# Linear attention and a routed expert per sequence: output tiles split by feature parity, expert weights kept in fixed slots with a conditional load, first expert product in halves, and another order list

## The chip, the cores and the metric

The kernel runs on one core of one Trainium2 chip. The metric is the device time of one execution in microseconds (us); lower is better. A core has a matmul engine (TensorE, PE in the profile, with weight loads as PEld), a vector engine (VectorE, DVE), a scalar engine (ScalarE, ACT), GpSimd (POOL), which issues all the loads here, and SyncE (SP), which issues the stores. Each engine takes its instructions in the order in which the program gives them to it.

## The reference, cut to what matters

For each of 8 sequences: 8 heads of linear attention (k^T v, then q times that), a root-mean-square norm over each head's 64 features, then a mean over the 576 positions that chooses one of 8 experts, and that expert's two products.

```python
batch, n_heads, seq, head_dim = (8, 8, 576, 64)
kv = np.einsum('bhsd,bhse->bhde', k, v)
out = np.einsum('bhsd,bhde->bhse', q, kv)
rms = np.sqrt(np.mean(out * out, axis=-1, keepdims=True) + 1e-06)
x = out / rms * g_norm                          # to (8, 576, 512)
logits = x.mean(axis=1) @ w_gate                # (8, 8 experts)
e_idx = np.argmax(logits, axis=1)
h = np.maximum(x[mask] @ w1[e], 0.0)            # 512 -> 1024
out[mask] = gate_w[mask, None, None] * (h @ w2[e])   # 1024 -> 512
```

With the inputs as they are drawn, the eight sequences choose experts 4, 4, 7, 6, 5, 1, 3, 1. Sequence 1 so repeats the expert of the one before it, and sequence 7 that of sequence 5.

## The kernel before, in words

All inputs are float32 in memory and are turned into float16 on the way in by the loads (GpSimd's queue); sums stay in float32. The program is a list of small steps, ORDER (lines 18 to 47), run in that order at build time; a step's name is two letters, then the sequence and an index. Every engine gets its instructions in the order of the list, so the list is the schedule; nothing is reordered later.

Loads: `lq` (line 93), `lk` (97), `lv` (103). The values v go into one of three block-diagonal buffers `vbd`, two heads to a block, with zeros that `zero_v` (129) writes once. `wl` (247) reads the chosen expert's index into a GpSimd register and loads both weight matrices, 1 MB each as float16, into a pool with three buffers.

Attention of one sequence: `tr` (134) transposes q, 18 matmuls; `te` (146) copies the result out of PSUM as qT (VectorE). `kv` (157) forms k^T v with 36 matmuls of 128 rows, 64 columns and 128 streamed columns, half of which are the zeros of `vbd`; `kc` (167) copies it to float16 (three VectorE casts). `ou` (176), for each of four pairs of heads `c`, multiplies with q on four 64x64 quarters of the array; its streamed operand steps through qT by 128 elements (256 bytes) from one column to the next:

```python
s["qT"][rs].rearrange("p j (h n) -> p h n j", h=H)[:, 2 * c + h]
```

`sq` (188, ScalarE) squares the result, `oc` (194, VectorE) copies it, `me` (199) takes the mean over the features with a matmul, `ln` (206, ScalarE) does a logarithm and an exponential, `xt` (213, VectorE) scales into xT. There are four of each per sequence. `ga`, `gb`, `gc` (223 to 245) form the logits and the index; `gb` is a small float32 matmul that needs all four `xt`. `ge` (258) forms the gate.

Expert of one sequence: `m1` (268) has eight steps of eight matmuls of 288 columns into a two-bank PSUM tile, `re` (279, ScalarE) takes 576 columns out of it; `m2` (286) has four steps of eight matmuls of 512 columns and one of 32 small ones (128 rows by 32 columns, line 301); `ev` (306, VectorE) scales two of the four at a time and SyncE stores them.

PSUM is one pool with two tags, "a" (attention) and "m" (expert), each of two tiles of two banks.

The list does the attention of sequences 0 and 1 first, then in each stage the expert of sequence b with the attention of sequence b + 2 woven between its steps, and at the end the experts of 6 and 7 alone. Loads of sequence b + 2 stand behind the weights of sequence b on GpSimd's queue, and those wait for the index of sequence b. At a stage's end `gb` of sequence b + 2 stands on TensorE's queue behind all of `m2` but its last step.

Of the kernel before, what the change touches and what calls it, by code (L numbers as in the profile page):

```python
# [24 lines left out]
sq21 oc21 re04 me20 m105 ln20 xt20 re05 me21 m106 ln21 xt21 re06 ou22 sq22 m107 oc22 re07 ou23
sq23 m200 oc23 m201 me22 ln22 ev00 xt22 me23 m202 ln23 m203 xt23 ga2 ev01 gb2 m204 gc2 wl2 ev02
ge2 lk4 lv40 lv41 lq4 m110 tr30 te30 re10 tr31 te31 m111 tr32 re11 te32 kv30 m112 kv31 re12 kc3
ou30 m113 sq30 oc30 re13 ou31 m114 sq31 oc31 re14 me30 m115 ln30 xt30 re15 me31 m116 ln31 xt31
re16 ou32 sq32 m117 oc32 re17 ou33 sq33 m210 oc33 m211 me32 ln32 ev10 xt32 me33 m212 ln33 m213
xt33 ga3 ev11 gb3 m214 gc3 wl3 ev12 ge3 lk5 lv50 lv51 lq5 m120 tr40 te40 re20 tr41 te41 m121  # L30
# [12 lines left out]
m251 me72 ln72 ev50 xt72 me73 m252 ln73 m253 xt73 ga7 ev51 gb7 m254 gc7 wl7 ev52 ge7 m160 re60
m161 re61 m162 re62 m163 re63 m164 re64 m165 re65 m166 re66 m167 re67 m260 m261 ev60 m262 m263
ev61 m264 ev62 m170 re70 m171 re71 m172 re72 m173 re73 m174 re74 m175 re75 m176 re76 m177 re77
m270 m271 ev70 m272 m273 ev71 m274 ev72
"""


@with_exitstack  # L50
def kernel(
    ctx: ExitStack,
    tc: tile.TileContext,
    q: bass.AP,
    k: bass.AP,
    v: bass.AP,
    g_norm: bass.AP,
# [10 lines left out]
    P = 128  # L68
# [290 lines left out]
```

## Time and profile before

| what | value |
|---|---|
| median of 3 runs | 249.75 us (249.34 to 250.88) |
| the profiled execution, its own time | 249.76 us |
| its span, first to last instruction | 248.0 us |
| time around the span | 1.76 us |
| TensorE busy | 196.9 us, 79% |
| VectorE / ScalarE busy | 111.6 us, 45% / 105.1 us, 42% |
| read from memory / written | 61.88 MB / 9.44 MB |

The profile shows one execution. Busy time of TensorE counts a matmul to its modelled end, so runs of matmuls overlap. In a windows view, the DMA columns give the mean busy share of the 16 DMA engines and what they moved (loads count as float16 there). The chain of waits is followed back from the last instruction, at each step to what released it.

### The profile page before, as it was taken

Reading aid. Unit: us, or ns where it says so; the run is one execution under the profiler, and the core shown is the slowest. Engines: PE = TensorE matmul, PEld = TensorE weight load, DVE = VectorE, ACT = ScalarE, POOL = GpSimd, SP = SyncE. Lnnn points to the kernel's source line nnn. Section 1 sums busy time; section 2 is a strip of 40 time slices with the busy share of each in tenths; the row PEclk is TensorE's granted clock in tenths of the full one; section 3 lists DMA queues with packets and bytes.
Section 4 is the critical chain, followed back from the end, with each engine's and each line's share of the span. In section 5 each row is a group of like instructions: output and inputs, shape, how many; then the busy total and the mean of one; then the engine's idle time right before and its main releaser. Section 6 shows DMA issues by size and latency. Waiting matters only on the chain.

```text
span 248.0 us, 4062 instructions
## 1 busy us (share of the span) xinstructions
PE 196.9 (79%) x1664; PEld 123.0 (50%) x1664; DVE 111.6 (45%) x235; ACT 105.1 (42%) x177; POOL 32.8 (13%) x54
## 2 busy tenths in 40 slices
PE   0355366358899889978998899889997999999990
PEld 0231151036554656464646564557455645957840
DVE  6625535532446535573357236733574358022031
ACT  2007405711484249413951385328542654622600
POOL 7100060041000500032002300140002000200000
PEclk9999999999999999999999999999999999999998
DMA  4996049999992699949995999599969902995023
GB/s 37 201 207 128 0 74 215 204 161 211 207 183 85 145 215 207 245 121 209 208 220 176 183 208 214 204 168 210 213 204 170 202 1 104 202 215 201 2 87 107
DMA packets 20644, 40.65 MB, mean 164 GB/s; under 512 B 2194, under 2 KB 11410, under 8 KB 20626
## 3 DMA queue, kind: packets, MB, share of 16 engines
q0 software_dynamic: 16128, 30.94, 69.1%
q1 hardware_dynamic: 4498, 9.46, 10.6%
q8 instruction: 13, 0.21, 0.3%
q14 instruction: 5, 0.04, 0.0%
HBM read 61.88 MB, written 9.44 MB: 288 GB/s over the span
## 4 chain that ended last, share of the span: by engine, by line
PE 61%; DMA 12%; DVE 11%; ACT 9%; issue 3%; POOL 2%; DVEq 0%; POOLq 0%
PE ps_m L275 27%; PE ps_m L294 14%; DMA qt<-in_q_dram 7%; PE ps_a L183 6%; DMA kt<-in_k_dram 5%; ACT ln L209 4%; ACT ln L211 4%; PE ps_a L162 4%; PE ps_a L144 3%; DVE xT L218 2%; PE ps_m L301 2%; PE ps_a L203 2%; DVE qT L149 2%; DVE kv L173 1%; DVE kv L172 1%
## 5 line engine op out<-in xcount | busy, mean ns | idle before, releaser
L275 PE MATMUL ps_m<-xT,w 128*128 128x288 f16 x512 | 74.0, 293 | 0.4 <-DVE ot L312 0.4
L275 PEld LDWEIGHTS <-w 128*128 128x128 f16 x512 | 56.0, 116 | 16.4 <-issue 10.5
L281 ACT ACTIVATE hT<-ps_m 128x576 f16<-128x576 f32 x64 | 41.5, 648 | 46.4 <-PE ps_m L275 46.3
L294 PE MATMUL ps_m<-w,hT 128*128 128x512 f16 x256 | 57.6, 379 | 0.0
L218 DVE SCALAR_TENSOR_TENSOR xT<-o,gcol,ln 128x576 f16<-128x576 f32 x32 | 26.2, 818 | 30.6 <-ACT ln L211 30.6
L294 PEld LDWEIGHTS <-hT 128*128 128x128 f16 x256 | 24.5, 98 | 30.2 <-issue 2.8
L312 DVE TENSOR_SCALAR ot<-ps_m,gates 128x1024 f32<-128x1024 f32 x16 | 20.5, 1281 | 34.3 <-PE ps_m L294 34.3
L191 ACT ACTIVATE sq<-ps_a 128x576 f16<-128x576 f32 x32 | 20.4, 650 | 36.0 <-PE ps_a L183 36.0
L197 DVE COPY o<-ps_a 128x576 f32<-128x576 f32 x32 | 23.9, 756 | 20.6 <-ACT sq L191 20.6
L183 PE MATMUL ps_a<-qT,kv 64*64 64x288 f16 x128 | 26.0, 651 | 7.7 <-DVE kv L171 4.2
L209 ACT ACTIVATE ln<-ps_a,eps 128x576 f32<-128x576 f32 x32 | 23.5, 734 | 19.2 <-PE ps_a L203 19.2
L252 POOL DMA_DIRECT2D w<-in_moe_w_dram x8 | 6.0, 754 | 178.9 <-PE ps_a L144 86.6
L144 PE MATMUL ps_a<-ident,qt 128*128 128x128 f16 x144 | 14.4, 253 | 17.1 <-DMA qt<-in_q_dram 10.3
L211 ACT ACTIVATE ln<-ln 128x576 f32<-128x576 f32 x32 | 21.9, 685 | 1.0
L144 PEld LDWEIGHTS <-qt 128*128 128x128 f16 x144 | 11.9, 116 | 19.2 <-DMA qt<-in_q_dram 10.8
L203 PE MATMUL ps_a<-sq,ones 128*128 128x288 f16 x64 | 13.9, 320 | 5.3 <-DVE o L197 5.2
L162 PE MATMUL ps_a<-vbd,kt 128*64 128x128 f16 x288 | 13.1, 250 | 5.7 <-DVE qT L152 3.1
L149 DVE COPY qT<-ps_a 128x1024 f16<-128x1024 f16 x16 | 11.0, 690 | 11.6 <-PE ps_a L144 11.6
L162 PEld LDWEIGHTS <-kt 128*64 128x64 f16 x288 | 11.3, 129 | 8.0 <-issue 4.5
L183 PEld LDWEIGHTS <-kv 64*64 64x64 f16 x128 | 4.7, 109 | 19.4 <-issue 7.3
L171 DVE CAST kv<-ps_a 128x256 f16<-128x256 f32 x8 | 3.4, 424 | 22.2 <-PE ps_a L162 22.2
L264 ACT ACTIVATE lg<-lg 128x8 f32<-128x8 f32 x8 | 1.7, 208 | 26.3 <-DVE lg L261 26.3
(36 smaller groups left out, 89.5 us busy)
## 6 DMA issues: line engine op xcount, KB each, us to landing
w<-in_moe_w_dram POOLq DMA_DIRECT2D x16, 1024.0 KB, 10.7
out_dram<-ot SPq DMA_DIRECT2D x16, 512.0 KB, 2.8
qt<-in_q_dram POOLq DMA_DIRECT2D x8, 576.0 KB, 18.6
vbd<-in_v_dram POOLq DMA_DIRECT2D x16, 288.0 KB, 15.9
kt<-in_k_dram POOLq DMA_DIRECT2D x8, 576.0 KB, 15.0
out_dram<-ol SPq DMA_DIRECT2D x32, 32.0 KB, 2.1
gcol<-in_g_norm_dram SPq DMA_DIRECT2D x1, 0.5 KB
wg<-in_moe_w_gate_dram SPq DMA_DIRECT2D x1, 16.0 KB, 8.0
```

The costliest lines, as they stand in the source:

```text
L144: nc.tensor.transpose(dst, s["q"][:, j, :], cs["ident"])
L162: nc.tensor.matmul(s["pk"][64 * g:64 * g + 64, 0, n * P:(n + 1) * P], s["k"][:, c, j, :], vbd[b % 3][:, c, :, j * Dh:(j + 1) * Dh], start= ...
L183: nc.tensor.matmul(po[64 * h:64 * h + 64, r, 0:HS], s["kv"][rs, col + 64 * h:col + 64 * h + 64], s["qT"][rs].rearrange("p j (h n) -> p h n ...
L191: nc.scalar.activation(t.rearrange("p (i n) -> p i n", i=2), s["po", c][:, :, 0:HS], AF.Square)
L197: nc.vector.tensor_copy(t.rearrange("p (i n) -> p i n", i=2), s["po", c][:, :, 0:HS])
L209: nc.scalar.activation(t.rearrange("p (i n) -> p i n", i=2), s["pm", c][:, :, 0:HS], AF.Ln, bias=cs["eps"])
L211: nc.scalar.activation(t, t, AF.Exp, scale=-0.5)
L218: nc.vector.scalar_tensor_tensor(out=s["xT"][:, c, :], in0=s["o", c], scalar=cs["gcol"], in1=s["ln", c], op0=ALU.mult, op1=ALU.mult, accum ...
L275: nc.tensor.matmul(ph[:, i, 0:HS], s["w1"][:, c, f // 4, :, f % 4], s["xT"][:, c, i * HS:(i + 1) * HS], start=(c == 0), stop=(c == NC - 1))
L281: nc.scalar.activation(s["hT"][:, f, :].rearrange("p (i n) -> p i n", i=2), s["ph", f][:, :, 0:HS], AF.Relu)
L294: nc.tensor.matmul(po[:, t % 2, :], s["hT"][:, f, c0:c0 + P], s["w2"][:, f // 4, f % 4, :], start=(f == 0), stop=(f == 7))
L312: nc.vector.tensor_scalar(out=ot, in0=po, scalar1=gate, scalar2=None, op0=ALU.mult)
```

## The change

Nine things change together.

1. **Tiles by parity.** `ou` now makes, for four heads and one parity of the feature number, a 128-row tile from eight matmuls of 64 rows by 32 columns, and qT is stored head by head so that its 288 columns lie side by side. A tile `c` holds four heads; tiles 2C and 2C+1 hold the two parities, so `me` adds both in PSUM, and `me` and `ln` run twice per sequence and not four times. `sq` and `oc` read PSUM in steps of 16 elements. `gcol` and the gate weights are laid out by parity.
2. **k^T v on quarters.** `vbd` and its zeros go; v is loaded like k in one DMA; `kv` is 72 matmuls of 64 rows, 64 columns and 64 streamed columns. `kc` moves to ScalarE.
3. **Weights in slots.** The weight pool becomes two constant buffers with three slots. `cw` (new, VectorE) reads the index into a VectorE register and copies 128x4096 float16 from the slot of the previous sequence (or of the one before it, if that one has the same expert) into this sequence's slot. The load (`wl` for w1, `wm` for w2) is then issued with a condition and is skipped where the expert repeats. There are 14 copies; with these inputs 2 of 8 sequences skip, 4 DMAs of 16.
4. **w1 by 2 rows.** A weight load reads runs of 8 KB of w1 and not 4 KB.
5. **First product in halves.** `m1` and `re` work on one half of the 576 columns: 128 `re` of 288 columns and not 64 of 576.
6. **PSUM.** Tag "a" keeps two tiles of two banks; a pool "m" has four tiles of one bank, also used by `gb` and `m2`; `ev` takes 512 columns at a time.
7. **Gate in three steps.** `ge` becomes `g1`, `g2`, `g3`.
8. **Filler.** `du` (new) issues 46 matmuls of 512 columns on zeros in the first part of the program.
9. **Another order.** ORDER is a new list, found by a search, in which steps of three sequences are mixed; the attention of sequence 2 stands before most of the expert of sequence 0, and `m1` of the next sequence begins among the `m2` of the one before.

```diff
 ORDER = """
...
+me00 oc01 tr10 tr11 ln00 te10 du1 ou03 du2 ou02 sq03 lk1 lv1 oc03 sq02 du2 me01 oc02 tr12 kv1
...
-            s["qT"] = att.tile([P, 18, P], F16, tag="qT", name="qT")
+            s["qT"] = att.tile([P, H, 18, 16], F16, tag="qT", name="qT")
...
+    def kv(b):
+        s = st[b]
+        for c in range(2):
+            for j in range(9):
+                for g in range(2):
+                    for i in range(2):
+                        rs = slice(64 * i, 64 * i + 64)
+                        nc.tensor.matmul(s["pk"][64 * g:64 * g + 64, i, c * Dh:(c + 1) * Dh],
+                                         s["k"][rs, 2 * g + c, j, :],
+                                         s["v"][rs, 2 * g + c, j, :],
+                                         start=(j == 0), stop=(j == 8))
...
+        nc.scalar.copy(s["kv"][:, 0], src)
+        nc.scalar.copy(s["kv"][0:64, 1], src[64:128])
+        nc.scalar.copy(s["kv"][64:128, 1], src[0:64])
...
     def ou(b, c):
...
+        for h in range(4):
+            for r in range(2):
+                rs = slice(64 * r, 64 * r + 64)
+                nc.tensor.matmul(po[32 * h:32 * h + 32, r, 0:HS],
+                                 s["kv"][rs, (c // 2 + r) % 2, h // 2, h % 2, c % 2:Dh:2],
+                                 s["qT"][rs, 4 * (c // 2) + h].rearrange("p j n -> p (j n)"),
+                                 start=True, stop=True)
+
+    def rows(po):
+        return po[:, :, 0:HS].rearrange("p r (j n) -> p r n j", n=16)
...
+    def me(b, C):
+        s = st[b]
+        pm = s["pm", C] = psum2()
         for i in range(2):
+            for j in range(2):
+                nc.tensor.matmul(pm[:, i, 0:HS], cs["ones"],
+                                 s["sq", 2 * C + j][:, i * HS:(i + 1) * HS],
+                                 start=(j == 0), stop=(j == 1))
...
+    def du(n):
+        t = psum1()
+        for i in range(n):
+            nc.tensor.matmul(t, cs["ident"], cs["junk"], start=True, stop=True)
...
+    def index(eng, b):
+        return eng.value_load(st[b]["ix"][0:1, 0:1]).with_bounds(min_val=0, max_val=E - 1)
+
+    def cw(b, n):
+        s = st[b]
+        if n == 1:
+            e = s["e"] = index(nc.vector, b)
+            s["src"] = (b - 1) % 3
+            if b > 1:
+                far = (e == st[b - 2]["e"]) * (e != st[b - 1]["e"])
+                s["src"] = (far * ((b - 2) % 3 - (b - 1) % 3) + (b - 1) % 3).with_bounds(
+                    min_val=0, max_val=2)
+        if b > 0:
+            w = cs["w1"] if n == 1 else cs["w2"]
+            nc.vector.tensor_copy(w[:, b % 3:b % 3 + 1, :], w[:, ds(s["src"], 1), :])
...
+            new = (ev != st[b - 1]["ev"]) * (ev != st[b - 2]["ev"])
+        s["new"] = {} if b == 0 else dict(cond=new, bounds_check="skip_entire_dma")
+        w1 = cs["w1"][:, b % 3, :]
...
-        ph = s["ph", f] = psum("m")
+        ph = s["ph", f, i] = psum1()
...
+        nc.scalar.activation(s["hT"][:, f, i * HS:(i + 1) * HS], s["ph", f, i][:, 0:HS],
+                             AF.Relu)
```

On GpSimd, near the program's start, the kernel before issues the loads of sequences 0 and 1, then waits for the index of sequence 0 (`TENSOR_LOAD ix`), and only behind the weights do the loads of sequence 2 follow:

```order
L105 DMA vbd_85<-in_v_dram 64x4x576 x2
L95 DMA qt<-in_q_dram 128x2304
L249 TENSOR_LOAD ix [waits DVE_49]
L249 ISA x2
L252 ISA
L252 DMA w_273<-in_moe_w_dram 128x4x1024 [waits DMASW0_49]
L254 ISA
L254 DMA w_274<-in_moe_w_dram 128x2x2048 [waits DMASW1_49]
L101 DMA kt<-in_k_dram 128x4x576 [waits DMASW2_49]
```

The changed kernel at the same place:

```order
L110 DMA vt<-in_v_dram 128x4x576
L106 DMA qt<-in_q_dram 128x2304
L110 DMA kt<-in_k_dram 128x4x576
L110 DMA vt<-in_v_dram 128x4x576 [waits DMASW0_49]
L278 TENSOR_LOAD ix [waits DVE_49]
L304 ISA
L304 DMA w_112<-in_moe_w_dram 128x2x2048 [waits DMASW1_49]
L106 DMA qt<-in_q_dram 128x2304 [waits DMASW2_49,PE_49]
L312 ISA
L312 DMA w_113<-in_moe_w_dram 128x2x2048 [waits DMASW3_49]
```

The three loads of sequence 2 moved ahead of the wait for the first index; only w1 stands directly behind it, with the next q ahead of w2.

On TensorE at the end of a stage, the kernel before has the gate's matmul (L233) between the last of the full `m2` matmuls (L294) and the small ones (L301):

```order
L294 LDWEIGHTS hT
L294 MATMUL ps_m<-w_754,hT 128x512
L233 MATMUL ps_a<-pr,onef 128x32 [waits DVE_49,Activation_49]
L301 LDWEIGHTS hT
L301 MATMUL ps_m<-w_754,hT 32x256
```

In the changed kernel the gate's matmul (L261) of one sequence stands in the middle of another's `m1` (L337):

```order
L198 MATMUL ps_a<-qT,kv 32x288
L337 LDWEIGHTS w_112
L337 MATMUL ps_m<-xT,w_112 128x288 [waits Activation_49]
L337 LDWEIGHTS w_112
L337 MATMUL ps_m<-xT,w_112 128x288
L261 MATMUL ps_m<-pr,onef 128x32 [waits DVE_49,Activation_49]
L337 LDWEIGHTS w_112
L337 MATMUL ps_m<-xT,w_112 128x288 [waits Activation_49]
```

The steps that lead up to the gate (`me`, `ln`, `xt`) now lie among matmuls of two experts, and the gate's matmul comes later in the list than it did.

On VectorE the changed kernel has, after each index, a register load and the two copies of a whole weight slot (L291) among the copies out of PSUM (L216, L373):

```order
L278 TENSOR_LOAD ix [waits DVE_49]
L291 REGISTER_ALU x2
L291 ISA
L291 COPY w_112<-w_112 128x4096 [waits DMASW1_49]
L216 COPY o<-ps_a 128x576 [waits Activation_49]
L216 COPY o<-ps_a 128x576 [waits PE_49,Activation_49]
L216 COPY o<-ps_a 128x576 [waits PE_49]
L373 TENSOR_SCALAR ot<-ps_m,gates 128x512 [waits DMAHW5_49,DVE_49]
L291 REGISTER_ALU x2
L291 ISA
L291 COPY w_113<-w_113 128x4096 [waits DMASW2_49]
```

Nothing of this stood on VectorE before; each copy waits for the load of the previous sequence's weights, and this sequence's load waits for the copy.

## Rows read from the trace of the kernel before

**Rows 1.** Page, part 1: busy us (share of the span) xinstructions.

```profile
PE 196.9 (79%) x1664; PEld 123.0 (50%) x1664; DVE 111.6 (45%) x235; ACT 105.1 (42%) x177; POOL 32.8 (13%) x54
```

**Rows 2.** Windows, one full stage: us, busy of each engine, clock, DMA share, GB/s.

```profile
108.46:134.12 25.66, 23.36 (x211) 14.57 (x209) 13.13 (x28) 12.88 (x23) 4.00 (x6) 1.00 0.96 198
```

**Rows 3.** Timeline of the first 60 us: start us, us, engine, line, operation [idle before <-releaser].

```profile
14.64 2.13 PE L162 MATMUL ps_a<-vbd,kt 128*64 128x128 f16 x36 [2.67 <-DMA kt<-in_k_dram]
...
31.31 0.16 DVE L245 FIND_INDEX8 ix<-mx,lg 128x8 uint32<-128x8 f32 x1
...
32.96 0.75 POOL L252 DMA_DIRECT2D w<-in_moe_w_dram  x1 [25.80 <-DVE qT L149]
...
54.31 1.03 PE L144 MATMUL ps_a<-ident,qt 128*128 128x128 f16 x8 [1.37 <-DMA qt<-in_q_dram]
```

**Rows 4.** Windows of one microsecond, columns as in rows 2.

```profile
24.00:25.00 1.00, 0.00 (x0) 0.00 (x0) 1.00 (x3) 0.95 (x2) 0.00 (x0) 1.00 0.00 0
...
116.00:117.00 1.00, 1.00 (x9) 0.77 (x8) 0.03 (x1) 0.65 (x1) 0.00 (x0) 1.00 1.17 223
...
132.00:133.00 1.00, 1.00 (x34) 0.78 (x34) 0.96 (x3) 0.00 (x0) 0.00 (x0) 1.00 0.03 12
```

**Rows 5.** The view of the weight tiles: their loads, from issue to landing.

```profile
DMA to landing us min/median/max: 7.8/10.7/13.6
```

**Rows 6.** Chain of waits in one stage: start us, us, what.

```profile
113.57 0.64 PE ps_a L162 x18
114.23 0.42 DVE kv L171
...
119.29 0.98 PE ps_m L275 x8
...
121.49 0.59 PE ps_a L183 x4
122.08 1.11 PE ps_m L275 x8
...
127.61 0.75 ACT ln L209
...
132.03 0.99 PE ps_m L301 x32
```

**Rows 7.** Chain of waits at the end, the expert of sequence 6.

```profile
209.98 7.96 PE ps_m L275 x64
217.94 6.92 PE ps_m L294 x32
```

**Rows 8.** Groups by line: names, shapes, xcount | busy us, mean ns of one | idle before.

```profile
L275 PE MATMUL ps_m<-xT,w 128*128 128x288 f16 x512 | 74.0, 293 | 0.4 <-DVE ot L312 0.4
...
L281 ACT ACTIVATE hT<-ps_m 128x576 f16<-128x576 f32 x64 | 41.5, 648 | 46.4 <-PE ps_m L275 46.3
...
L183 PE MATMUL ps_a<-qT,kv 64*64 64x288 f16 x128 | 26.0, 651 | 7.7 <-DVE kv L171 4.2 <-DVE kv L173 1.9 <-ACT ln L209 1.7
...
L312 DVE TENSOR_SCALAR ot<-ps_m,gates 128x1024 f32<-128x1024 f32 x16 | 20.5, 1281 | 34.3 <-PE ps_m L294 34.3
...
L162 PEld LDWEIGHTS <-kt 128*64 128x64 f16 x288 | 11.3, 129 | 8.0 <-issue 4.5 <-DMA kt<-in_k_dram 2.9
...
L149 DVE COPY qT<-ps_a 128x1024 f16<-128x1024 f16 x16 | 11.0, 690 | 11.6 <-PE ps_a L144 11.6
...
L301 PE MATMUL ps_m<-w,hT 128*32 128x256 f16 x256 | 8.5, 274 | 0.0
...
L317 DVE TENSOR_SCALAR ol<-ps_m,gates 128x256 f32<-128x256 f32 x8 | 3.8, 475 | 0.0
...
L152 DVE COPY qT<-ps_a 128x256 f16<-128x256 f16 x8 | 2.3, 288 | 3.4 <-PE ps_a L144 3.4
```

**Rows 9.** Timeline of the last stage's end.

```profile
241.06 1.06 PE L301 MATMUL ps_m<-w,hT 128*32 128x256 f16 x32
...
242.92 2.10 SPq L321 DMA_DIRECT2D out_dram<-ol  x4
```

More of the change, by code (lines that the diff above doesn't have):

```diff
@@ L25 @@
[L25 to L30, printed above, removed]
@@ L119, in setup @@
         nc.vector.memset(s["ones"], 0.0)
-        nc.vector.memset(s["ones"][0:64, 0:64], 1.0 / Dh)
-        nc.vector.memset(s["ones"][64:128, 64:128], 1.0 / Dh)
+        for i in range(4):
+            nc.vector.memset(s["ones"][32 * i:32 * i + 32, 32 * i:32 * i + 32], 1.0 / Dh)
         s["onef"] = const.tile([P, P], F32, name="onef")
@@ L157, in kv @@
-    def kv(b, n):
-        s = st[b]
-        for j in range(9):
-            for g in range(2):
-                c = 2 * g + n
-                nc.tensor.matmul(s["pk"][64 * g:64 * g + 64, 0, n * P:(n + 1) * P],
-                                 s["k"][:, c, j, :],
-                                 vbd[b % 3][:, c, :, j * Dh:(j + 1) * Dh],
-                                 start=(j == 0), stop=(j == 8))
+        if i == 0:
+            src = s["pt"].rearrange("p i (j h n) -> p (i j) h n", h=H, n=16)
+        else:
+            src = s["pk"].bitcast(F16)[:, 0, 512:512 + 2 * P].rearrange(
+                "p (j h n) -> p j h n", h=H, n=16)
@@ L176, in ou @@
+        nc.scalar.copy(s["kv"][0:64, 1], src[64:128])
+        nc.scalar.copy(s["kv"][64:128, 1], src[0:64])
     def ou(b, c):
         s = st[b]
[L178 to L186 removed]
+        po = s["po", c] = psum2()
@@ L258, in ge @@
-    def ge(b):
-        s = st[b]
-        lg, mx = s["lg"], s["mx"]
-        nc.vector.tensor_scalar(out=lg, in0=lg, scalar1=mx[:, 0:1], scalar2=None,
+        ev = s["ev"] = index(nc.gpsimd, b)
+        new = None
+        if b == 1:
+            new = ev != st[0]["ev"]
+        elif b > 1:
+            new = (ev != st[b - 1]["ev"]) * (ev != st[b - 2]["ev"])
+        s["new"] = {} if b == 0 else dict(cond=new, bounds_check="skip_entire_dma")
+        w1 = cs["w1"][:, b % 3, :]
+        s["w1"] = w1.rearrange("p (c f) -> p c f", c=NC)
@@ L271, in m1, with g3 @@
+    def g3(b):
+        nc.vector.reciprocal(cs["gates"][:, b:b + 1], st[b]["gs"])
+    def m1(b, f, i):
+        s = st[b]
+        if f == 0 and i == 0:
             s["hT"] = hp.tile([P, 8, S], F16, tag="hT", name="hT")
-        ph = s["ph", f] = psum("m")
+        ph = s["ph", f, i] = psum1()
         for c in range(NC):
-            for i in range(2):
-                nc.tensor.matmul(ph[:, i, 0:HS], s["w1"][:, c, f // 4, :, f % 4],
-                                 s["xT"][:, c, i * HS:(i + 1) * HS],
-                                 start=(c == 0), stop=(c == NC - 1))
```

227 lines of the change are left out of this document (114 added, 113 removed).

## The prediction, made before the changed kernel was run

> **What bounds the kernel now.** I read the page's busy times first. TensorE is busy 79% of the span, VectorE 45% [rows 1]: TensorE leads, and a fifth of the span has no matmul. Where that fifth lies the windows and the timeline say. A full stage (the expert of one sequence, the attention of another) takes 25.66 us, with TensorE busy 23.36 of them [rows 2], so only 2.3 us idle. The rest is at the start. k^T v of sequence 0 begins at 14.64, its index is known at 31.47, its weights are issued at 32.96, and the steady stages begin when q of sequence 2 lands, at 54.31 [rows 3]. In between the DMA engines do nothing for about ten microseconds, as from 24 to 25 [rows 4], since the loads of sequence 2 stand behind the wait for that index. The 36 matmuls of k^T v span 2.13 us there and about 1.28 in a stage [rows 3, 6], though the granted clock column reads 1.00 in both; no term below is taken from those slow rows.
>
> So there are three places to gain: the start, the waits in six stages, and the matmuls of attention. The expert's matmuls are a floor: 7.96 + 6.92 [rows 7] + 0.99 for the small ones [rows 6] = 15.87 us a sequence, 127.0 for eight. Attention with its drains is the rest of a stage's busy time: 23.36 - 15.87 = 7.49 us.
>
> **The output tiles (saved).** Four matmuls of line 183 take 0.59 us [rows 6], sixteen 2.36. One is 651 ns long; one of line 275 is 293, of which it streams 0.98 / 8 = 122, so 171 are its end [rows 6, 8]. Line 183 then streams 480 ns for the same 288 columns: all four quarters run at once, each at a quarter of the pace. Line 301 (four column tiles, operand side by side) is 274 long, so streams 256 columns in 103, at full pace, and 32 of them take 0.99, 31 ns each [rows 6, 8]: four at once there too. What differs is the step of 256 bytes, and the change removes it. Eight matmuls at 31 ns by 288 / 256 are 0.28 us, four tiles 1.1. Bounds: all eight at once, 0.15 a tile, 0.6; none at once, 8 x 0.147 (0.59 / 4), 4.7. I take 1.1, from the row with the same column tiles: 1.25 saved.
>
> **k^T v on quarters (added).** Eighteen matmuls now take 0.64 us [rows 6], 36 ns each, 1.28 for all. There will be 72, with half the columns. Below: half the time each, 1.28, nothing lost; above: 36 each, 2.6. I take 31, the shortest spacing of load and matmul that a row shows [rows 6]: 2.2, so 0.9 added.
> The Trainium skill, TensorEngine Tiling (Array Packing), Performance Considerations, speaks against this edit: a matmul carries about 60 cycles whatever its columns, and a factor should not be taken from a dimension that is already small. At the 2.4 GHz level that is an estimate of 25 ns, 1.8 us for 72. It agrees in sign with the row of 31 ns, and the sum would be 2 us lower by it over five attentions.
>
> **Waits and drains.** About four times a stage TensorE stands behind a copy, such as the casts of kv (0.42 each, three in a row, [rows 6]) or the chain that ends in the gate ahead of line 301. Each leaves a modelled end of 0.17 in the busy time, 0.7 in all. The new list puts matmuls of two experts into these places. I let 0.7 of busy and 1.8 of the 2.3 idle go and keep 0.5 a stage. Attention then costs 7.49 - 0.7 - 1.25 + 0.9 = 6.45 us. Changing tile shape costs something: eight matmuls of line 275 take 1.11 behind line 183 and 0.98 otherwise [rows 6]; that 0.13 is in the 7.49, and the new list changes shape about as often.
>
> **VectorE.** It was busy 13.13 us in a stage [rows 2]. Off: the kv casts, 1.27. On: the stores' scaling in halves, 475 + 256 x 1.05 = 744 ns instead of half of 1281 (1.05 ns an element is the slope between lines 312 and 317, [rows 8]), 0.4 for two pairs; qT in one copy, 0.15 less at the slope of lines 149 and 152, 0.52 ns [rows 8], 0.9 more at 1.05; reading the index, at most the 1.49 us that GpSimd took from index to issue [rows 3]; and two copies of 4096 elements. No row shows a float16 copy from SBUF to SBUF. At 0.52 ns it is 2.3 us, at 1.05 it is 4.4, at no less than zero below; I take 2.3, from the only float16 copies there are. Sum 18.2 of a stage of about 22.8: not the bound, though its queue has little air.
> The Trainium skill, VectorE: DVE Perf Modes, Rules for kernel authors, gives a dense 16-bit copy within SBUF four elements a cycle; at 0.96 GHz that is an estimate of 1.1 us a copy and 15.8 a stage. No run here shows it yet.
>
> **ScalarE** had 12.88 [rows 2]. Sixteen `re` of 288 columns instead of eight at 648 ns [rows 8] lie between 0 more (half the time each) and 5.2 more (no shorter); three casts add 1.3, and two of four `ln` pairs go. Even with 5.2 and nothing taken off it is 19.4 of 22.8, and its work lies under matmuls.
>
> **Loads.** At 132 to 133, before a stage ends, the DMA engines are idle at 0.03 [rows 4]: the loads are done by then. Four weight loads of sixteen fall away, and no stage waits for them now, so they are worth nothing by themselves; they make up for stages becoming shorter. At 198 GB/s [rows 2] a stage moves 5.1 MB, 22.8 us at the 223 of the busy row [rows 4], just a new stage; the skipped weights of sequence 1 (2.1 MB, 9 us) give the lead.
>
> **The start.** The loads of sequence 2 fill the gap and are there by about 31 us, so its attention is mostly done before the weights arrive. The first index: two `ln` pairs fewer on the chain (the logarithm 0.75 [rows 6], the exponential about as long, so some 1.45 each), but transposes, a qT copy (1.2), k^T v (2.2) and casts (1.3) of sequence 1 now stand ahead of the gate on the same queues, so 31.47 - 2.9 + 4.7 = 33.3. Issue 1.49 later, landing 7.8 after issue [rows 3, 5]: 42.6. I take 43.0 for the first expert matmul (40 to 48). The filler matmuls stand where TensorE waits for loads; I cost them at nothing. Were that cover gone, 46 of 512 columns are 46 x 0.216 (6.92 / 32, [rows 7]) = 10 us.
>
> **The sum.** Start 43.0; experts 127.0; attention left after the start, all of sequences 3 to 7 and a third of 2: 5.35 x 6.45 = 34.5; waits 7 x 0.5 = 3.5; from the last matmul (242.12) to the end of the span 5.9 [rows 9]. Span 213.9. The profiled execution took 249.76 with a span of 248.0, so 1.8 more: 216. Its own time is the median of the runs to 0.01 us.
>
> **Rivals.**
> *The copies hold VectorE.* If a weight copy takes 4.4 us, VectorE has 22.4 of 22.8 and TensorE, with two attention tiles, waits for `oc`. Fourteen copies are 29 us more; half on the path gives 231. For it: the slope of 1.05 on every float32 row, the wait of each copy for the previous weights. Against: the float16 slope.
> *Everything overlaps.* No waits left, 0.6 for the tiles, 1.28 for k^T v, start 1.5 earlier: 216 - 3.5 - 5.35 x 1.4 - 1.5 = 203. For it: line 301 shows tiles at full pace. Against: every stage has five hand-overs between engines.
> *Slower: each small matmul pays for its weight load.* A load of 64 columns lasts 129 ns [rows 8]. If it can't run under matmuls of other quarters, each pair costs 129 more. On the path are 5.35 x 104 pairs and the two k^T v ahead of the first index, 700: 90 us, 306 in all. It decides from 34 / 700 = 49 ns on top, 80 ns a pair. For it: eight quarter tiles are new here. Against: 36 ns at line 162 with those same loads.
> *The skip does nothing* (condition false, or the copies wasted in five of seven cases): the loads are hidden anyway, so still 216, unless the loads then bind, some 9 us, 225.
>
> **How the numbers follow.** Forecast 0.47, by itself 209 to 223; VectorE held 0.25; everything overlaps 0.20; the pieces cancel to within 1% of before (about what a measurement of this kernel can tell from no change) 0.03; slower 0.05. So faster by over 1%: 0.92. The range 203 to 232 leaves out the last two, and the far side of the first rivals.
>
> **What would show it.** Right: no empty DMA stretch between 22 and 33 us; first expert matmuls near 43; `ou` matmuls near 290 ns long, not 651; 72 k^T v matmuls in about 2.2 us; stages of 21 to 23 us; weight copies near 2.3 us. Wrong: TensorE waits on `oc` behind a weight copy (first rival); k^T v of 6 us or more (slower); first expert matmul after 48, or waits for weights in stages 3 to 5, which would say that the loads have become the bound.

## The result and the profile after

The changed kernel takes 208.2 us (median of four executions, 206.75 to 208.77), the kernel before 249.5 in the same rounds: a ratio of 0.833, 95% interval 0.827 to 0.838. The forecast was 216.0, its range 203 to 232. The profiled execution took 206.75 us with a span of 205.1.

The head of the page and the busy times [rows 1]: TensorE does 18 us less and still fills 87% of the span.

```profile
span 205.1 us, 5085 instructions
...
PE 178.8 (87%) x2126; PEld 118.2 (58%) x2126; DVE 109.8 (54%) x230; ACT 99.0 (48%) x233; POOL 26.1 (13%) x46
```

The timeline of the first 45 us answers to [rows 3]:

```profile
14.31 0.78 PE L177 MATMUL ps_a<-vt,kt 64*64 64x64 f16 x72
...
31.13 0.16 DVE L273 FIND_INDEX8 ix<-mx,lg 128x8 uint32<-128x8 f32 x1
...
32.52 0.70 POOL L304 DMA_DIRECT2D w<-in_moe_w_dram  x1 [23.00 <-DVE o L216]
...
42.10 3.10 PE L337 MATMUL ps_m<-xT,w 128*128 128x288 f16 x24
```

The first index comes hardly earlier than before (31.29 against 31.47), and the first weights are issued at 32.5 instead of 33.0. What is new is how much is done by 42.10, when the first expert matmul starts: the attention of sequences 0 and 1, and about half of that of sequence 2. The windows cut at the first expert matmul and at the last matmul (columns as in [rows 2]) then divide the span:

```profile
0.00:42.10 42.10, 26.50 (x415) 14.27 (x416) 17.26 (x43) 15.48 (x27) 9.65 (x19) 0.92 0.95 165
42.10:198.85 156.75, 152.26 (x1713) 103.97 (x1711) 92.01 (x187) 83.54 (x207) 16.45 (x27) 0.99 0.86 184
198.85:205.10 6.25, 0.00 (x0) 0.00 (x0) 0.48 (x1) 0.00 (x0) 0.00 (x0) 0.88 0.35 110
```

In the 156.75 us in the middle TensorE stands still for only 4.5. In the kernel before, one stage of 25.66 had 2.3 of it [rows 2]. The chain of waits in that part runs almost throughout from matmul to matmul, where [rows 6] went through casts, a logarithm and the gate:

```profile
83.25 0.70 PE ps_a L177 x72
83.96 1.83 PE ps_m L354 x8
...
86.77 0.25 PE ps_a L198 x8
...
87.64 0.99 PE ps_m L360 x32
```

Here stand the two prices that the prediction had to bound: 72 matmuls of k^T v in 0.70 us (line 177) and one output tile in 0.25 (line 198). The groups by line [rows 8] of the changed kernel:

```profile
L337 PE MATMUL ps_m<-xT,w 128*128 128x288 f16 x512 | 73.3, 291 | 3.4 <-DMA w<-in_moe_w_dram 2.7 <-ACT hT L343 0.7
...
L216 DVE COPY o<-ps_a 128x576 f32<-128x576 f32 x32 | 23.6, 752 | 7.1 <-ACT sq L210 7.0
L210 ACT ACTIVATE sq<-ps_a 128x576 f16<-128x576 f32 x32 | 20.4, 651 | 20.5 <-PE ps_a L198 18.2 <-DVE o L216 2.2
L291 DVE COPY w<-w 128x4096 f16 (+1 forms) x14 | 17.0, 1223 | 4.9 <-DVE ix L273 2.9 <-issue 1.3 <-DVE lg L318 0.7
...
L198 PE MATMUL ps_a<-qT,kv 64*32 64x288 f16 x256 | 9.4, 299 | 4.2 <-DVE qT L166 3.5 <-ACT kv L189 0.7
...
L177 PE MATMUL ps_a<-vt,kt 64*64 64x64 f16 x576 | 6.2, 194 | 1.0 <-DVE qT L166 1.0
```

A weight copy (line 291) takes 1.223 us. Taking the output tile out of PSUM in steps of 16 elements (lines 210 and 216) costs nothing: 651 and 752 ns, against 650 and 756 for the same two operations before.

Four waits make nearly all of the 4.5: 1.04 us for a copy of q ahead of 60.45, 2.25 for the weights of sequence 2 ahead of 77.10, 0.43 for weights ahead of 103.53 and 0.69 for ScalarE ahead of 107.26. GpSimd's timeline shows what stands ahead of the longest:

```profile
48.48 0.04 POOL L304 DMA_DIRECT2D w<-in_moe_w_dram  x1 [13.22 <-DMA w<-in_moe_w_dram]
...
56.14 0.04 POOL L312 DMA_DIRECT2D w<-in_moe_w_dram  x1 [6.37 <-DMA w<-in_moe_w_dram]
56.74 0.54 POOL L106 DMA_DIRECT2D qt<-in_q_dram  x1 [0.56 <-issue]
...
65.89 0.70 POOL L304 DMA_DIRECT2D w<-in_moe_w_dram  x1 [7.32 <-DVE gates L327]
```

The two skipped loads of sequence 1 take 0.04 us each (a load that is issued takes 0.70), but GpSimd stands in front of them until 48.5 and 56.1, when the copies into their slots are done, and loads that need no index stand behind them: one behind the first, three behind the second. So from 55 to 60 us the DMA engines are nearly idle. At 75 us TensorE waits and then works at a lower clock (the column behind the busy times: 1.00 is the level of 2.4 GHz, 0.50 that of 1.2, a value between them a stretch with both):

```profile
55.00:60.00 5.00, 4.41 (x25) 2.30 (x24) 3.27 (x6) 1.63 (x6) 1.87 (x4) 1.00 0.38 57
...
75.00:80.00 5.00, 2.90 (x13) 1.92 (x14) 2.66 (x7) 1.44 (x5) 0.00 (x0) 0.72 1.17 216
```

On the chain this is the landing of 11.16 us and two groups of matmuls behind it, 2.99 us for twelve that take 1.47 elsewhere and 2.07 for eight that take 1.73. How much of this wait comes from the empty stretch, the runs with loads moved ahead show below:

```profile
65.89 11.16 DMA w<-in_moe_w_dram
77.10 2.99 PE ps_m L337 x12
80.09 2.07 PE ps_m L354 x8
```

### The profile page after: what moved, and what is told of

Its sections match the earlier page's. It is cut to its first block, busy times and chain, and to the rows that moved or that the text cites. A ratio compares the mean times of both kernels' runs of the same rounds, so it can differ in the third digit from the quotient of the medians.

```text
span 205.1 us, 5085 instructions
## 1 busy us (share of the span) xinstructions
PE 178.8 (87%) x2126; PEld 118.2 (58%) x2126; DVE 109.8 (54%) x230; ACT 99.0 (48%) x233; POOL 26.1 (13%) x46
## 3 DMA queue, kind: packets, MB, share of 16 engines
q0 software_dynamic: 12864, 26.74, 73.3%
HBM read 61.88 MB, written 9.44 MB: 348 GB/s over the span
## 4 chain that ended last, share of the span: by engine, by line
PE 74%; DMA 9%; DVE 6%; ACT 5%; issue 3%; DVEq 0%; ACTq 0%; POOLq 0%
PE ps_m L337 29%; PE ps_m L354 26%; DMA w<-in_moe_w_dram 5%; PE ps_a L223 4%; DMA qt<-in_q_dram 3%; PE ps_m L360 3%; PE ps_m L248 3%; PE ps_a L157 3%; PE ps_a L198 3%; DVE xT L239 2%; DVE qT L166 2%; PE ps_a L177 2%; ACT ln L230 1%; ACT ln L232 1%; ACT kv L189 1%
## 5 line engine op out<-in xcount | busy, mean ns | idle before, releaser
L337 PE MATMUL ps_m<-xT,w 128*128 128x288 f16 x512 | 73.3, 291 | 3.4 <-DMA w<-in_moe_w_dram 2.7
L343 ACT ACTIVATE hT<-ps_m 128x288 f16<-128x288 f32 x128 | 48.2, 412 | 39.3 <-PE ps_m L337 36.8
L337 PEld LDWEIGHTS <-w 128*128 128x128 f16 x512 | 56.3, 116 | 14.2 <-DMA w<-in_moe_w_dram 3.5
L373 DVE TENSOR_SCALAR ot<-ps_m,gates 128x512 f32<-128x512 f32 x32 | 23.8, 749 | 38.5 <-PE ps_m L354 38.4
L216 DVE COPY o<-ps_a 128x576 f32<-128x576 f32 x32 | 23.6, 752 | 7.1 <-ACT sq L210 7.0
L166 DVE COPY qT<-ps_a 128x256 f16<-128x256 f16 (+1 forms) x16 | 11.9, 755 | 27.2 <-PE ps_a L177 15.3
L291 DVE COPY w<-w 128x4096 f16 (+1 forms) x14 | 17.0, 1223 | 4.9 <-DVE ix L273 2.9
L230 ACT ACTIVATE ln<-ps_a,eps 128x576 f32<-128x576 f32 x16 | 11.9, 742 | 11.4 <-PE ps_a L223 11.1
L248 PE MATMUL ps_m<-junk,ident 128*128 128x512 f16 x46 | 14.7, 443 | 0.0
L198 PE MATMUL ps_a<-qT,kv 64*32 64x288 f16 x256 | 9.4, 299 | 4.2 <-DVE qT L166 3.5
L232 ACT ACTIVATE ln<-ln 128x576 f32<-128x576 f32 x16 | 10.9, 684 | 0.5
L198 PEld LDWEIGHTS <-kv 64*32 64x32 f16 x256 | 3.5, 90 | 12.2 <-issue 9.3
L223 PEld LDWEIGHTS <-ones 128*128 128x128 f16 x64 | 6.5, 104 | 4.6 <-issue 1.8
## 6 DMA issues: line engine op xcount, KB each, us to landing
qt<-in_q_dram POOLq DMA_DIRECT2D x8, 576.0 KB, 12.5
```

The lines of the kernel that those rows point to most:

```text
L198: nc.tensor.matmul(po[32 * h:32 * h + 32, r, 0:HS], s["kv"][rs, (c // 2 + r) % 2, h // 2, h % 2, c % 2:Dh:2], s["qT"][rs, 4 * (c // 2) + h ...
L216: nc.vector.tensor_copy(t.rearrange("p (r n j) -> p r n j", r=2, n=16), rows(s["po", c]))
L223: nc.tensor.matmul(pm[:, i, 0:HS], cs["ones"], s["sq", 2 * C + j][:, i * HS:(i + 1) * HS], start=(j == 0), stop=(j == 1))
L248: nc.tensor.matmul(t, cs["ident"], cs["junk"], start=True, stop=True)
L291: nc.vector.tensor_copy(w[:, b % 3:b % 3 + 1, :], w[:, ds(s["src"], 1), :])
L337: nc.tensor.matmul(ph[:, 0:HS], s["w1"][:, c, c0:c0 + 509:4], s["xT"][:, c, i * HS:(i + 1) * HS], start=(c == 0), stop=(c == NC - 1))
```

## The experiments

### Parts of the change, put alone into the kernel before

**Loads of sequence 2 ahead of the first index.**

```diff
-lq0 zv0 lv00 lv01 lk0 cs zv1 zv2 lk1 lv10 lv11 lq1 tr00 te00 tr01 te01 tr02 te02 kv00 kv01 kc0
+lq0 zv0 lv00 lv01 lk0 cs zv1 zv2 lk1 lv10 lv11 lq1 lk2 lv20 lv21 lq2 tr00 te00 tr01 te01 tr02 te02 kv00 kv01 kc0
...
-ln02 xt02 me03 ln03 xt03 ga0 gb0 gc0 wl0 ge0 lk2 lv20 lv21 lq2 tr10 te10 tr11 te11 tr12 te12
+ln02 xt02 me03 ln03 xt03 ga0 gb0 gc0 wl0 ge0 tr10 te10 tr11 te11 tr12 te12
```

> The kernel before with one edit of its list: the four loads of sequence 2 stand ahead of the wait for the first index. Theory (the early start of the changed kernel, 42.1 us instead of 54.3, comes mostly from mixing the attention of sequences 0 and 1, and the loads alone free only the last wait): the attention of sequence 1 still ends at 50.4, so the stages begin near 52 and the time falls by 2 to 3 us, to about 247. Rival (the loads alone are what held the start): the stages begin near 43 and the time falls by about 10 us, to 239 to 240.

Measured: 247.7 us, ratio 0.992 (0.990 to 0.995), so 1.8 us: the first matmul of sequence 2 moves from 54.31 to 52.55. The idle DMA stretch of [rows 4] is filled and gives only that: the loads alone were not what held the start.

**q stored head by head.**

```diff
-            s["qT"] = att.tile([P, 18, P], F16, tag="qT", name="qT")
+            s["qT"] = att.tile([P, H, 18, 16], F16, tag="qT", name="qT")
...
-                                 s["qT"][rs].rearrange("p j (h n) -> p h n j", h=H)
-                                 [:, 2 * c + h], start=True, stop=True)
+                                 s["qT"][rs, 2 * c + h].rearrange("p j n -> p (j n)"),
+                                 start=True, stop=True)
```

> The kernel before with qT stored head by head, so that line 183 streams columns that lie side by side; the results come out of PSUM in steps of 16. Nothing else. Theory (the step of 256 bytes made the four quarters stream at a quarter of the pace): the matmul of line 183 falls from 651 to about 290 ns, four of them from 0.59 to about 0.2 us, a stage by 1.2 to 1.8 us and the time by 8 to 12 us, to 238 to 242. Rival (four quarters share one read path, whatever the step): it stays at 651 ns and the time within 1 us of before; if reading PSUM in steps costs, sq and oc get longer and the time goes up.

Measured: 244.0 us, ratio 0.977 (0.972 to 0.982), so 5.5 us, less than the 8 to 12 expected. The group of line 183, with the same 64x64 quarters and the same 288 columns, now side by side:

```profile
L183 PE MATMUL ps_a<-qT,kv 64*64 64x288 f16 x128 | 13.5, 340 | 10.6 <-DVE kv L173 4.4 <-DVE kv L171 4.2 <-ACT ln L212 2.1
```

The mean falls from 651 ns [rows 8] to 340, so the step of 256 bytes was the cause, not the quarters. The group is 12.5 us less busy, and 5.5 arrive: it waits 10.6 us now, where it waited 7.7, for casts and logarithms that come no sooner.

**k^T v on quarters**, in two halves as that kernel's list has it.

```diff
-                nc.tensor.matmul(s["pk"][64 * g:64 * g + 64, 0, n * P:(n + 1) * P],
-                                 s["k"][:, c, j, :],
-                                 vbd[b % 3][:, c, :, j * Dh:(j + 1) * Dh],
-                                 start=(j == 0), stop=(j == 8))
+                for i in range(2):
+                    rs = slice(64 * i, 64 * i + 64)
+                    nc.tensor.matmul(s["pk"][64 * g:64 * g + 64, i, n * Dh:(n + 1) * Dh],
+                                     s["k"][rs, 2 * g + n, j, :], s["v"][rs, 2 * g + n, j, :],
+                                     start=(j == 0), stop=(j == 8))
```

> The kernel before with k^T v on quarters alone: v dense, 72 matmuls of 64x64 with 64 columns, no zero blocks, casts still on VectorE, old list. Theory (quarters run four at once and a pair of load and matmul needs only 10 ns, as the changed kernel shows with 72 in 0.75 us): k^T v in a stage falls from 1.3 to about 0.75 us, the time by 3 to 5 us, to 245 to 247. Rival (the old list hides it, since the next step waits for the casts and the copies anyway): within 1 us of before.

Measured: 247.0 us, ratio 0.988 (0.983 to 0.993), so 2.5 us. Two pieces of the chain in one stage:

```profile
86.12 0.48 PE ps_a L162 x36
86.59 1.10 PE ps_m L274 x8
87.70 0.45 PE ps_a L162 x36
```

36 small matmuls take less than the 18 large ones did, 0.64 [rows 6]: some 0.35 us an attention, 2.8 for eight. The run also loads v in one piece and writes no zeros. Its first expert matmul comes at 48.93 instead of 50.84, but the first matmul of sequence 2 still waits for its q, until 54.50 (54.31 before), so the start gives nothing. The edit that the prediction charged 0.9 us an attention saves by itself.

### The list

**All parts of the change, with the list of before** (its steps in their old order, no filler).

```diff
-lq0 lk0 lv0 cs tr02 tr00 tr01 du9 du4 kv0 te01 te00 kc0 du4 ou00 ou01 sq00 lq1 oc00 sq01 du4
...
+lq0 lv0 lk0 cs lk1 lv1 lq1 tr00 tr01 te00 tr02 te01 kv0 kc0 ou00 sq00 oc00 ou01 sq01 oc01 me00
+ln00 xt00 xt01 ou02 sq02 oc02 ou03 sq03 oc03 me01 ln01 xt02 xt03 ga0 gb0 gc0 cw01 wl0 cw02 wm0
...
```

> The changed kernel with the list of before: each step put where its counterpart stood, no filler, the two weight copies ahead of their loads, the loads of sequence 2 behind the first index again. All other parts of the change stay. Theory (the list gives the larger half: the start and the waits at the gate): stages of 23 to 24 us instead of 25.7, first expert matmul at 45 to 50, time 225 to 235, so that list and filler are worth 17 to 27 of the 41 us. Rival (the cheaper steps give nearly all and the list little): 210 to 216.

Measured: 238.8 us, ratio 0.956 (0.951 to 0.961). The parts bring 10.7 us, the new list with its filler the other 30.6, more than the 17 to 27 expected. The split holds for this order of the two; the new list without the parts was not run. With the old list the first expert matmul comes at 46.70 (42.10 with the new one) and the last matmul ends at 231.98, 185.3 later (156.75). Of these 28.5 us, idle time of TensorE makes 18.9: 183.50 - 160.16 = 23.3 us of it in the window that begins with the first expert matmul, 4.5 in the corresponding one above.

```profile
46.50:230.00 183.50, 160.16 (x1783) 107.04 (x1784) 92.53 (x184) 85.86 (x208) 17.67 (x29) 0.99 0.75 160
```

What TensorE waited for in that kernel (us in total, times, the longest):

```profile
PE ps_a L157 <- DMA qt<-in_q_dram: 21.9, 6, 8.7
...
PE ps_m L337 <- DVE ol L381: 4.1, 2, 2.4
PE ps_a L198 <- ACT kv L187: 3.9, 8, 0.5
...
PE ps_a L198 <- ACT kv L189: 3.6, 8, 0.5
```

The 8.7 of the first row is the load at the program's start. Behind the first expert matmul there are five waits for a q, 13.3 us; two for the copy of the small output tile (line 381), 4.1; and those for the casts of k^T v in six sequences, 5.8. Together they are 23.2 of the 23.3. Each q is the last of five loads that GpSimd issues one behind another, the weights first, which wait for their index and, from sequence 1 on, for the copies. What the copies do to line 381 the chain at a stage's end shows:

```profile
71.21 0.75 ACT ln L230
...
78.40 1.22 DVE w L291
79.62 0.39 DVE ol L381
...
82.05 0.81 PE ps_a L177 x72
```

From 71.2 to 82.0 no matmul is on the chain. TensorE has others to do for most of it and stands still for 1.64 us, until the copy of the small output tile, which stands behind two weight copies on VectorE, is done at 80.0.

**The same, with the loads of sequence 2 ahead.**

```diff
-lq0 lv0 lk0 cs lk1 lv1 lq1 tr00 tr01 te00 tr02 te01 kv0 kc0 ou00 sq00 oc00 ou01 sq01 oc01 me00
+lq0 lv0 lk0 cs lk1 lv1 lq1 lk2 lv2 lq2 tr00 tr01 te00 tr02 te01 kv0 kc0 ou00
...
```

> The parts of the changed kernel with the list of before, and in that list the loads of sequence 2 moved ahead of those steps of sequence 0 that lead to its index. TensorE waited there 4.6 us for q of sequence 2 from 48.8 to 53.4, and about 2 us in four later stages, which this edit leaves. Theory (the list's worth lies mostly in steps mixed between sequences, not in where the loads stand): 232 to 236 us against 238.8. Rival (the early loads carry most of the list's 30 us): 225 or less.

Measured: 234.1 us, ratio 0.938 (0.934 to 0.941), 4.7 us less, as the theory had it. In the kernel before the same edit gave 1.8: where the loads stand at the start is worth 2 to 5 us. Some 26 us remain: steps of several sequences mixed, filler, and where the later loads stand. TensorE still stands still for 18.3 us behind its first expert matmul (4.5 in the changed kernel): 6.4 in three waits for a q, 5.6 for line 381 and 5.8 for the casts. No run takes these apart.

**No filler.**

```diff
-lq0 lk0 lv0 cs tr02 tr00 tr01 du9 du4 kv0 te01 te00 kc0 du4 ou00 ou01 sq00 lq1 oc00 sq01 du4
+lq0 lk0 lv0 cs tr02 tr00 tr01 kv0 te01 te00 kc0 ou00 ou01 sq00 lq1 oc00 sq01 me00 oc01 tr10 tr11 ln00 te10 ou03 ou02 sq03 lk1 lv1 oc03 sq02 me01 oc02 tr12 kv1
...
```

> The changed kernel without its 46 filler matmuls. Theory (they keep TensorE at its higher clock level through the first 40 us and cost little): without them the matmuls of the start run at half pace until the experts are under way, the first expert matmul comes at 43 to 45 instead of 42.1, the time rises by 1 to 4 us, to 209 to 212. Rival (the filler lies on the path, as the chain shows it with 3% of the span, and gives nothing back): the time falls by 1 to 4 us.

Measured: 210.4 us, ratio 0.844 (0.839 to 0.848), 2.2 us slower than the changed kernel in its first four executions and 1.0 slower than in the six taken later (below), where the intervals of the ratios overlap: 0.839 to 0.848 here, 0.838 to 0.843 there. So the filler gains 1 to 2 us at most, and that is not clear of the spread. From 40 to 45 us, where the first expert matmuls start, the clock is 0.68 of full speed:

```profile
40.00:45.00 5.00, 2.55 (x25) 1.38 (x26) 5.00 (x11) 1.71 (x5) 0.00 (x0) 0.68 1.05 213
```

The first 24 matmuls of line 337 take 4.14 us there, 3.10 with filler. So the filler hides behind waits, as was predicted, and may give a little through the clock; it cannot be much of the 30.6 us.

### Copies and skipped loads

**No copies, all eight pairs loaded.**

```diff
-        s["new"] = {} if b == 0 else dict(cond=new, bounds_check="skip_entire_dma")
+        s["new"] = {}
...
-            w = cs["w1"] if n == 1 else cs["w2"]
-            nc.vector.tensor_copy(w[:, b % 3:b % 3 + 1, :], w[:, ds(s["src"], 1), :])
+        return
```

> The changed kernel without the weight copies and without the condition: all eight pairs of weights are loaded into the three slots. Theory (loads are hidden when they are issued early, and each conditional load holds the queue for the copy ahead of it): the weights of sequence 1 take 10 us of the bus while the loads of sequence 4 wait; VectorE is 17 us freer; the time comes out within 3 us of the changed kernel, 206 to 211. Rival (the skipped 4 MB is what lets the stages shorten): 213 to 220, with waits for weights in several stages.

**Copies kept, all eight pairs loaded.**

```diff
-        s["new"] = {} if b == 0 else dict(cond=new, bounds_check="skip_entire_dma")
+        s["new"] = {}
```

> The changed kernel with its copies of weight slots but with every weight load issued, none skipped. Theory (the skip alone is what the eighth pair of weights costs, the copies lie beside other work): 214 to 217 us, within 1 us of the kernel without copies that loads all eight pairs (215.7). Rival (each load must wait for the copy into its slot, so copies cost as soon as the loads bind): 217 to 222.

Measured: 215.7 us without the copies (ratio 0.865, 0.859 to 0.870) and 222.4 with them (0.886, 0.881 to 0.892), both as the rivals had it and not the theories, the second just above its rival's 222. What TensorE waited for, without and with copies:

```profile
PE ps_m L328 <- DMA w<-in_moe_w_dram: 6.8, 4, 2.6
```

```profile
PE ps_m L337 <- DMA w<-in_moe_w_dram: 12.3, 3, 4.7
```

(us in total, times, the longest.) So the loads do bind when all sixteen are made: the skip is worth 6 to 7.5 us against a kernel that needs no copies, and 13 to 14 against one that copies anyway (by the two medians of the changed kernel, 208.2 and 209.4). The copies cost 6.7 us where no load is skipped. 5.5 of it is the longer wait for weights just shown, and the waits of TensorE for VectorE are the same in both, so it goes through the queue and not through VectorE's time: each load into a slot waits for the copy into it. GpSimd's rows for sequence 1, without copies and with them:

```profile
49.02 0.70 POOL L295 DMA_DIRECT2D w<-in_moe_w_dram  x1 [13.29 <-DVE ix L273]
...
50.47 0.71 POOL L303 DMA_DIRECT2D w<-in_moe_w_dram  x1
```

```profile
50.44 0.70 POOL L304 DMA_DIRECT2D w<-in_moe_w_dram  x1 [14.55 <-DVE w L291]
...
58.10 0.70 POOL L312 DMA_DIRECT2D w<-in_moe_w_dram  x1 [6.19 <-DVE w L291]
```

w2 is issued 7.6 us later, since its copy stands that much later in VectorE's order.

### Past the changed kernel

**Six loads moved ahead of the conditional ones of sequence 1**: k and v of sequence 3, q, k and v of sequence 4, q of sequence 5. (On GpSimd's queue v of sequence 3 stood ahead of them already, so five change places.)

```diff
-m1031 oc20 oc21 re001 wm0 re041 re010 m1050 me20 g30 ga1 re031 gb1 gc1 m1021 m1060 re050 m1030
-cw11 ou22 ln20 re021 ou23 lv3 m1020 re060 re030 m1040 wl1 re020 sq23 oc22 re040 m1011 m1070 xt20
...
+m1050 me20 g30 ga1 re031 gb1 gc1 m1021 m1060 re050 m1030 cw11 ou22 ln20 re021 ou23 m1020 re060
+re030 m1040 lv3 lk3 lq4 lv4 lk4 lq5 wl1 re020 sq23 oc22 re040 m1011 m1070 xt20 sq22 xt21
...
```

> The changed kernel with six loads (k, v of sequence 3, q, k, v of 4, q of 5) moved in the list ahead of the conditional loads of sequence 1; nothing else. Theory (the DMA engines fall to 57 GB/s from 55 to 60 us because the skipped loads of sequence 1 wait on GpSimd for the copies while loads that nobody holds stand behind them; so the weights of sequence 2 land only at 77 us, TensorE waits 2.25 us and then runs at the lower clock for 5 us): they land by 74 to 75, the wait goes, the time falls by 3 to 5 us, to 203 to 205. Rival (the weights are late because of their index, known at 63.6): they land at 77 again and the time is the same within 1 us.

Measured: 205.9 us, ratio 0.827 (0.820 to 0.833): 2.3 us below the changed kernel, but the intervals overlap. So both were timed again, in the same rounds.

> The changed kernel itself, timed once more beside the next one. Expected 206.7 to 208.8 us, as in its first four executions.

> The changed kernel with six loads of sequences 3 to 5 moved ahead of the conditional weight loads of sequence 1, once more and in the same rounds as the changed kernel. Theory (the wait of 2.25 us for the weights of sequence 2 is on the path, and its shortening counts): 1.5 to 3 us faster than the changed kernel in these rounds, with intervals apart. Rival (the time gained at 75 us is given back by a later wait or a lower clock): within 1 us.

Measured: the changed kernel 209.4 us (208.4 to 210.5), ratio 0.841 (0.838 to 0.843), 1.2 above its first median and just past what was expected of it; with the loads ahead 205.9 (204.0 to 208.5), ratio 0.824 (0.820 to 0.828). The intervals stand apart: 3.6 us, 1.7%. This version beats both kernels. Its windows:

```profile
55.00:60.00 5.00, 5.00 (x39) 3.42 (x37) 4.25 (x8) 1.78 (x7) 0.04 (x1) 1.00 1.16 205
65.00:70.00 5.00, 5.00 (x58) 3.62 (x43) 3.43 (x7) 2.66 (x8) 1.46 (x2) 1.00 0.46 82
75.00:80.00 5.00, 3.61 (x31) 2.27 (x30) 3.63 (x8) 1.96 (x6) 0.00 (x0) 1.00 1.15 247
80.00:85.00 5.00, 5.00 (x99) 3.18 (x98) 2.02 (x5) 3.02 (x7) 0.00 (x0) 1.00 1.06 213
```

The empty DMA stretch at 55 us is filled. It comes back smaller at 65, when the weights of sequence 2 still wait for their index and for the copy into their slot: they are issued at 67.43, at 67.38 in the changed kernel of the same rounds. They did not land by 74 to 75, as the theory of the first run had it, and a wait of 1.39 us stays, until 77.79 (2.33 there, until 78.68). So filling the empty stretch took 0.9 us off the wait; the rest stayed, with an issue that came no earlier. The lower clock behind the wait is gone: 1.00 from 80 to 85. The changed kernel in those rounds has 0.69 there:

```profile
80.00:85.00 5.00, 5.00 (x50) 2.67 (x52) 0.75 (x1) 1.14 (x4) 0.00 (x0) 0.69 1.18 214
```

Of the 2.6 us between these two spans (206.7 and 204.1) the clock is so the larger part, some 1.6 (0.31 of 5 us), and the wait the smaller.

**The same with ten more filler matmuls ahead of the first gate.**

```diff
-du3 gb0 oc10 oc11 ou12 sq12 gc0 g10 oc12 lq2 du1 ou13 lk2 sq13 du4 me10 oc13 me11
+du3 du6 du4 gb0 oc10 oc11 ou12 sq12 gc0 g10 oc12 lq2 du1 ou13 lk2 sq13 du4 me10
```

> As the kernel with six loads ahead, and ten more filler matmuls ahead of the first gate matmul, where TensorE waits for VectorE from 27.4 to 29.4 us. Theory (that gap lets the granted clock fall to 0.50 from 30 to 35 us, and filler, gate and means run at half pace there): the clock stays at 1.00, the first expert matmul comes at 40.5 to 41.5, and the time is 1 to 2 us below the one with the loads ahead, unless the first weights, issued at 32.5, bind at 40.5 to 41. Rival (the clock falls anyway, or the filler outlasts the gap): same or up to 2 us slower than the one with the loads ahead.

Measured: 206.0 us, ratio 0.825 (0.819 to 0.832), no change. Its windows:

```profile
30.00:35.00 5.00, 4.48 (x106) 2.64 (x106) 2.65 (x8) 3.41 (x6) 2.61 (x4) 1.00 0.35 40
...
40.00:45.00 5.00, 4.78 (x33) 2.30 (x18) 2.58 (x8) 2.49 (x7) 0.55 (x1) 0.50 1.06 215
```

The clock is full from 30 to 35, where the version without it had 0.50, and 0.50 from 40 to 45, where that had 0.75, behind a wait of 2.86 us for the copy of q: the slow stretch has moved, not gone. The first expert matmul comes at 41.61, behind a wait of 0.22 for its weights, so these nearly bind here.

## Why the prediction was right, and where it was off

The direction, the mechanism and the order of size held; the time is 8 us below the forecast, at the lower edge of the 209 to 223 that the prediction gave its main case (208.2, and 209.4 when timed again). In the prediction's own steps, by the span (213.9 forecast, 205.1 measured):

- **The start**: 43.0 forecast, 42.10 measured. The pieces were not all right: k^T v of sequence 1 was charged at 2.2 us and takes 0.77, and the index comes at 31.3, not 33.3. TensorE's order took that back: the chain there does not come from the weights but from the output tiles of sequence 2, which stand ahead of the first expert matmul and waited 2.42 us for a copy of q. The sign "no empty DMA stretch between 22 and 33 us" held up to 30: all loads of three sequences have landed by then, and from 30 to 35 the DMA engines are busy for 0.36 of the time.
- **The output tiles**: 1.1 us an attention forecast from the row with four column tiles, four times 0.25 measured, 299 ns a matmul. Right, and the experiment with q head by head shows the stride to be the cause.
- **k^T v on quarters** is the term that was mis-sized: 72 pairs of load and matmul were priced at 31 ns each, 2.2 us, and take 0.70, 9.7 ns each. The range given (1.28 to 2.6) missed it too: its lower end took half the time of a matmul with twice the columns and so assumed that no more of them run side by side than before. Four quarters work at once instead of two halves: 64 columns at the pace of line 275 (288 in 122 ns) take 27 ns, so at 9.7 ns a pair about three must stream at any time. Over 5.35 attentions it is 5.35 x 1.5 = 8.0 us, the size of the whole miss, and the sign was wrong: the edit saves 0.6 an attention. The overhead of about 60 cycles a matmul in the Trainium skill, TensorEngine Tiling (Array Packing), Performance Considerations, at 2.4 GHz an estimate of 25 ns, was no guide either: measured over all quarters together a pair costs 9.7 ns. It can hold for one quarter, where every fourth pair makes 39.
- **The slower rival** rested on a weight load that cannot run beside other quarters. It would have shown in the same row; it did not.
- **Waits**: 0.5 at each of seven hand-overs, 3.5, was forecast. There are 4.5 us without a matmul, and some 1.9 more at a lower clock, 6.4. The size is low by nearly half and the place is another: of hand-overs between engines two are left, 1.04 and 0.69, and nearly two thirds of it is one event, the late weights of sequence 2.
- **VectorE**: 2.3 us a weight copy forecast, 1.22 measured. The page VectorE: DVE Perf Modes of the Trainium skill (Rules for kernel authors) gave an estimate of 1.1, and the trace agrees with that. In 23 us of the steady part VectorE is busy 13 to 17 us, and TensorE waits for it once behind 42 us, so the rival in which the copies hold it fell. In the old list a weak form of it shows: there TensorE waits 4.1 us for the small output tile behind the copies.
- **The skipped loads**: "worth nothing by themselves" is what failed; that they make up for shorter stages held, and mattered more than was counted. The prediction counted 5.1 MB a stage against 22.8 us, just a new stage; a sequence came out at 156.75 / 8 = 19.6 us, below the 21 to 23 given as a sign, and with all loads made TensorE waits 6.8 to 12.3 us for weights (2.7 with the skip). The rival "the skip does nothing" put 9 us on this case, and 13 to 14 were measured; that its 225 lies near the 222.4 is in part luck, since it was added to a base that was 8 too high.
- **Experts and tail**: half of `m1` steps at 0.49 and `m2` at 1.73 as before; the tail 6.25 instead of 5.9.

In sum: 8.0 from k^T v and 0.9 from the start, 3.2 given back by waits and the tail, and a remainder of about 3, which must lie in drains and expert matmuls and was not measured by itself, make the 8.8 us between the two spans. "Everything overlaps" (203) came nearer to the time than the forecast, but not by its own parts: it had no waits and 0.6 for the tiles, where 6.4 and 1.0 were measured. Mainly k^T v, which went below even its 1.28, brought the time towards it.

What stays open: which of the list's moves carry the 26 us that remain when the loads at the start are taken off, 1 to 2 us of filler at most and 6.4 of waits for a later q among them. The halves of `m1`, the loads of w1 by 2 rows and the fewer `me` and `ln` were not tried by themselves.

## What to carry to other kernels

Price a packed matmul by how many tiles of the array work at once, not by the shortest spacing of a pair that another shape shows; and look at the step of the streamed operand before blaming the tile shape. An edit that shortens every stage can turn loads that were hidden into the bound, so price a skipped load at the new stage's length. A conditional load is cheap when it is skipped, but what stands behind it on its queue waits, as it does, for its index and for the copy into its slot: put unconditional loads ahead.

## What the runs showed of the hardware that was not expected

- Pairs of weight load and matmul on four 64x64 quarters follow each other at 9.7 ns (72 in 0.70 us), on two halves of 128x64 at 36. Of the eight 64x32 tiles of line 198, which together fill the array, four stream at a time: 8 matmuls of 288 columns take 0.25 us, 31 ns each, where 288 columns of line 275 stream in 122.
- On the same 64x64 quarters a matmul whose streamed operand steps by 256 bytes lasts 651 ns [rows 8], and 340 when it lies side by side; reading PSUM in steps of 64 bytes costs ScalarE and VectorE nothing.
- Behind an idle stretch of TensorE the granted clock can fall to the 1.2 GHz level while TensorE is busy again. In the changed kernel 1.98 us of idle time ahead of 29.44 are followed by 0.50 from 30 to 35; 2.42 ahead of 41.28 in the same execution are followed by 1.00:

```profile
30.00:35.00 5.00, 4.97 (x31) 2.25 (x31) 2.87 (x9) 2.02 (x3) 2.48 (x4) 0.50 0.36 40
...
40.00:45.00 5.00, 3.72 (x42) 3.10 (x43) 4.11 (x9) 3.10 (x9) 0.00 (x0) 1.00 1.05 212
```

A wait so can cost more than its length, but these runs give no rule for when it does, and where the lower level falls differs between executions of one kernel (0.72 at 75 to 80 in one, 0.69 at 80 to 85 in another).
- The page's row of memory read gives 61.88 MB with skipped loads and without; the queue's own row falls from 30.94 to 26.74 MB. The queue is the row to read where loads are conditional.
